# A gated linear scan with a top-2 mixture of adapters on one core: output rows of 8 KB, shorter early input rows, the masked logits on GpSimd, and a new order on every engine

## The chip, the cores and the metric

The kernel runs on one core of a Trainium2 chip. The metric is the time of one execution in device microseconds; the kernel before has a median of 201.33 us over three runs (201.27 to 201.44).

## The reference, cut to what matters

```python
# a, b: (8, 6400, 128) float32
h = zeros((8, 128))
for t in range(6400):                 # a linear scan along the sequence, per batch
    h = a[:, t] * h + b[:, t]
    x[:, t] = h
x = x.reshape(51200, 128)
logits = x @ w_gate                   # 8 experts
topk = argpartition(-logits, 2)[:, :2]
w = softmax of the two largest logits
out = x + sum over the two experts e of  w_e * ((x @ A[e]) @ B[e])    # rank 16
```

## The kernel before, in words

The 51200 tokens are 100 chunks of 512. `a` and `b` come from HBM with tokens on partitions; TensorE turns them so that the 128 features lie on partitions and the tokens along the row; VectorE runs the scan of a chunk along the row; TensorE multiplies with `A` and `w_gate`, the gate is worked out, and TensorE adds the chunk and its delta.

Each step has one letter, and the dictionary `ORDER` (line 24) spells out, for each engine, the order in which its steps are issued. No scheduler moves anything at run time: an engine issues its string from left to right and waits at each step for the semaphores of what that step needs. The steps are:

- **x, y (SyncE):** loads of `a` and `b`. `LOADS_A` (line 12) and `SEGMENTS` (line 11) give the chunks of each load. A load of m chunks lays 4m neighbouring tokens on one partition, so its rows in HBM are 2 KB times m: one chunk 2 KB, two chunks 4 KB, four chunks 8 KB. `a_tm` and `b_tm` hold 16 chunks each.
- **a, b, f (TensorE):** transposes of `a` (`solo_a`), of `b`, or of both together in alternation (f, in `front`). In the long middle part an f takes the `b` of chunk c and a half of two chunks of the `a` of the next four; `ahead` (line 415) says which. So the step f of chunk 88 needs the load of `a` of chunks 92 to 95.
- **a (ScalarE):** copies a transposed bank of `a` from PSUM to `a_st` (line 386).
- **s (VectorE):** the scan of one chunk, from `a_st` and from the PSUM bank of `b` (line 402), into `xT` in float16. The banks of `b` are `BANK_B` (line 16), the others rotate through `RING` (line 22).
- **z (TensorE, ScalarE):** `x @ [A, w_gate]` for up to three blocks of 128 tokens (line 500), copied to `zl` (line 506).
- **1 to 8, u, p, q, r:** the gate of a group of chunks (`GROUPS`, line 14; mostly six chunks), in `gating`: on VectorE the largest logit (1), its place (2), the logits with that place masked (3, line 536), the second largest (4) and its place (6); on GpSimd two differences (5, 8); on ScalarE one sigmoid (u); on GpSimd the two weights and their sum (p, q, r).
- **m (GpSimd or VectorE, as `MU` says, line 56):** the product of a chunk's `z` with its gate (line 588). **t (TensorE, then ScalarE or VectorE, as `TE` says, line 53):** the transpose of that product for two chunks and its copy (line 605).
- **d (TensorE), o (ScalarE):** chunk plus delta into PSUM (`out_chunk`, line 614), and the copy to `outt` (line 631), which holds 16 chunks.
- **o, p (SyncE):** the stores (`store`, line 648), with the chunks of `STORES` (line 13) in each. `BACKS` (line 20) says over how many chunks the tokens of an `xT` block are interleaved, which sets the row of a store: today 2 KB for the first and last four chunks, 4 KB for the rest. `SPLIT` (line 23) cuts one store in two by partitions.

All loads but one and all stores go through one queue, that of SyncE, in the order of its string. Where SyncE stands before a store that is not ready, the loads behind it are not issued.

Of the kernel before, what the change touches and what calls it, by code (L numbers as in the profile page):

```python
# [18 lines left out]
COLD, SOLO, FUSED, AE = {0: 1.95, 1: 1.3}, {1: 0.436, 2: 0.48}, {2: 0.59}, [0.592, 0.592]  # L19
BACKS = [1] * 4 + [2] * 46 + [1] * 4  # L20
ONE_SIGMOID, T_UNIT = True, 2
RING = [0, 3, 4, 5, 6, 7]
SPLIT = {20: [68]}
ORDER = {
    "pe": (
        "wbaabzzbazzbaaaazzaztffffzztzfdzzffzzfdfzfzzzffzzftzzffdzfdzzftzfzfzdfdzfzzzfzzfttzzffddtddzzfzfdzzf"
        "ztdffzzdtdffzztdzfdzzfdtzffzztddffzddtdffddzztzffzztzdffzdzztffzzzzdddtdtffzddztffzdzdfddfztzzffzdzd"
        "tffzzzddftzzzffdztzdftfddzftddffzzzdzfzdftzzffzztzddffdztzdtffzztddffddzzzfdzztzzfzdftzzfdtdffzzzddd"
        "ffdtztzffzzzddfdfttzdffazzdztdfddtzzzdzzddtafazdzzbtdzbzztddztdbzzadbdtddzdzdzttddtzddtdddtdtddddttd"
        "d"  # L30
    ),
    "act": (
        "ycciacazzazzuaaaazzuzaataaazztzzauaozzaazozaazzzzaazuatazzaoauzzoztzaazzaoazoazzzzzaauztzaaoooozzaza"
        "ozzazoaazzuootaazozzazoazozaazzutoaoazoouoaaoozzzaazztzoaazzozaazzzzooouoaazooztaazzoooaoazzzuaazzoo"
        "aazzzooazzzaaozztoautaoozaooaazzzoazzouazzaazzzooaaozztoaazzouoaaoozzzaozzzzzaoatzzauooaazzzoooaaozt"
        "zaauzzzaoooatzoaaazzuozooozzzoozzotaauzzzotozzzzoootzzauoouoozzotoztuoooztooooouuoooooo"
    ),
    "dve": (
        "ss12346ss123m4i61ss2s3s4s1s6s2s3s4s6s1s2s3s4s6sss1ss2s3s4sts16s2t3ss4sts1s62s3sts4sts1s263s4stssts6s"
        "ssts1s234tts1s263ss4ssts6sts1s2sts3s41s26s3sts4ss6sts1sts23sts4s6t1s2ssts13s4s2t6s3s4s6stss1s23sts4s"  # L40
        "m6tsts1m2m34s6ss1st12m3m4263s4ts1mm2m63m4mm6t1m21m32m34m4t66tmmtt"
    ),
    "pool": (
        "ccc85qpr85pqrmc855pqrmm8pqrmm85qprmmmm58mmqprmmmmm85mpqrmmmm85mmpqr58mmmmpmqmrmmmm85mmpqrmmm8m5mpqmr"
        "mmmmmm58qprmmm85mmmqprmmmmm58pmqrmmmmmm58pqrmm58mmmmqprmmmm58pqrmmm58qpmrmm58mq85prpq85pqrr8585ppqqr"
        "r"
    ),
    "sp": (
        "xxyxyxyxyxyxyyyxyyxyyxooyxyyoxyyyyyoxxoooyyxoyyyxoyxyooyyxoxopyoyyxoyyxyoooxyoyxyooyxyooyyxooyyxoyyx"
        "ooyxyoooyxoxxyyyoooyooooooooooooooooooo"  # L50
    ),
}
TE = (
    "aaaadaddaddaddadddadddaadddadddaddaadddaadadaadadddd"
)
MU = (
    "dpppppppppppppppppppppppppppppppppppppppppppppppppppppppppppppppppppppppppppdpdpdppppddpdddddddddddd"
# [144 lines left out]
def bass_associative_scan_2x2__then__mixture_of_adapters_kernel(  # L202
# [29 lines left out]
    with ExitStack() as stack:  # L232
# [54 lines left out]

        o_ms = P.add("pool", "c", [], lambda: eng["pool"].memset(ident_f[:, :], 0.0), dur=0.46)
# [20 lines left out]
        o_cB = P.add("pool", "c", [o_c[2]], lambda: eng["pool"].tensor_copy(B_h, cst_f[:, W:]), dur=0.38)  # L309

# [62 lines left out]
        def emptied(c, g, o, ba):  # L373
# [11 lines left out]
            e = P.add("act", "a", [o] + [ast_user[k % NA] for k in chunks] + [o_sg if c == 0 else None],  # L385
                      lambda: eng["act"].copy(dst, src()), dur=AE[0 if m == 1 else 1])  # L386
# [43 lines left out]
        def front(c):  # L430
# [3 lines left out]
            sl, q, m, h = place[0][c]  # L434
            if m == 1:
                solo_a(c, 0)
            elif (c - h, 0) not in o_A:
                for p in (0, 2):
                    for g in (0, 1):
                        solo_a(c - h + p, g)  # L440
            deps, ts = turned(1, c, bb)
            deps += user[bb.n]
            if c in ahead and place[0][c + 4][2] == 4:
                c1, g = ahead[c]
# [9 lines left out]
            elif c in ahead:  # L454
                if h % 2:
# [35 lines left out]
        def zlogits(b0, n):  # L491
# [10 lines left out]
            o = P.add("pe", "z", [scanned(b0 + n - 1), o_ch], zmm, dur=(0.059 if span[b0 // 4][1] == 1 else 0.062) * n, ring=bk, mm=n)  # L502
# [14 lines left out]
        def gating(gi, b0, nb):  # L517
# [17 lines left out]
            d3 = P.add("dve", "3", [d2],  # L535
                       lambda: eng["dve"].scalar_tensor_tensor(  # L536
                           out=ll, in0=kk1, scalar=-1.0e30, in1=Lp, op0=ALU.mult, op1=ALU.add),
                       dur=dur, lock=True)
# [20 lines left out]
            p1 = P.add("pool", "p", [a1, d2, d3] + free,  # L559
# [12 lines left out]
        def back(gi, c0, q0, n):  # L572
# [28 lines left out]
            te = "dve" if TE is None else {"a": "act", "d": "dve"}[TE[turn["t"]]]  # L601
# [12 lines left out]
        def out_chunk(c, e_t):  # L614
# [12 lines left out]
            o_D[c] = P.add("pe", "d", [e_t, o_cB], delta, dur=0.448 if span[c][1] == 1 else 0.48, ring=bo, mm=8, late=(1, [e_t, o_cB]))  # L627
            reads(b0, o_D[c])
            p0 = b0 % NO
            o_oe[c] = P.add("act", "o", [o_D[c]] + [out_user[p0 + k] for k in range(4)],  # L630
# [174 lines left out]
```

## Time and profile before

| | |
|---|---|
| time of the profiled execution | 201.33 us |
| its span, first to last instruction | 199.5 us |
| outside the span | 1.8 us |
| TensorE, VectorE, ScalarE, GpSimd busy | 91%, 89%, 89%, 64% |
| packets of SyncE's queue, as a share of 16 engines' span | 97.5% |
| bytes read and written in HBM | 52.56 MB, 26.21 MB |

The time is that of the execution from which the profile was taken, and it is also the median. The span is what the profile shows; the 1.8 us around it are the launch and the end. A busy share is the part of the span in which an engine has an instruction in work. The share of a queue is the time its packets took on the 16 DMA engines; where packets overlap, it goes over 100% in a stretch.

### The profile page before, as it was taken

Reading aid. Unit: us, or ns where it says so; the run is one execution under the profiler, and the core shown is the slowest. Engines: PE = TensorE matmul, PEld = TensorE weight load, DVE = VectorE, ACT = ScalarE, POOL = GpSimd, SP = SyncE. Lnnn points to the kernel's source line nnn. Section 1 sums busy time; section 2 is a strip of 40 time slices with the busy share of each in tenths; the row PEclk is TensorE's granted clock in tenths of the full one; section 3 lists DMA queues with packets and bytes.
Section 4 is the critical chain, followed back from the end, with each engine's and each line's share of the span. In section 5 each row is a group of like instructions: output and inputs, shape, how many; then the busy total and the mean of one; then the engine's idle time right before and its main releaser. Section 6 shows DMA issues by size and latency. Waiting matters only on the chain.

```text
span 199.5 us, 7518 instructions
## 1 busy us (share of the span) xinstructions
PE 181.4 (91%) x3137; PEld 165.1 (83%) x3137; DVE 177.8 (89%) x269; ACT 177.9 (89%) x384; POOL 128.2 (64%) x205
## 2 busy tenths in 40 slices
PE   2887988999999999999999989989999999898881
PEld 1766877888899999899998979978989899797770
DVE  0586789999999999999999988999999999999880
ACT  2476597999999999999999998989989999999872
POOL 1023006692798969966986794969888786665440
PEclk9995599999999999999999999999999999999999
DMA  6999999999999999999999999999999999999697
GB/s 185 401 405 415 414 412 413 414 414 404 419 410 420 409 416 418 410 420 407 420 413 407 415 418 417 419 411 418 417 408 418 411 409 407 412 389 369 268 365 272
DMA packets 21381, 79.26 MB, mean 397 GB/s; under 512 B 3427, under 2 KB 3555, under 8 KB 18403
## 3 DMA queue, kind: packets, MB, share of 16 engines
q1 hardware_dynamic: 19875, 78.39, 97.5%
q10 hardware_dynamic: 1472, 0.40, 0.9%
q8 instruction: 24, 0.39, 0.8%
q14 instruction: 10, 0.08, 0.1%
HBM read 52.56 MB, written 26.21 MB: 395 GB/s over the span
## 4 chain that ended last, share of the span: by engine, by line
PE 41%; DMA 23%; DVE 15%; ACT 13%; SPq 2%; issue 2%; POOL 2%; DVEq 0%; ACTq 0%
PE ps L768 22%; PE ps L772 19%; DMA a_tm<-in_a_dram 15%; DVE xT L402 9%; DMA b_tm<-in_b_dram 8%; ACT zl L506 4%; ACT outt L631 4%; ACT a_st L386 4%; DVE zw L588 4%; SPq L335 2%; ACT zwT L605 1%; DVE zwT L605 1%; POOL g L562 1%; DVE k L534 0%; DVE L L536 0%
## 5 line engine op out<-in xcount | busy, mean ns | idle before, releaser
L402 DVE TENSOR_TENSOR_SCAN xT<-a_st,xT,ps 128x512 f16<-128x512 f32 x96 | 120.1, 1251 | 7.1 <-PE ps L768 5.3
L588 POOL TENSOR_TENSOR zw<-zl,g 128x512 f16<-128x512 f32 x82 | 85.9, 1071 | 9.8 <-PE ps L768 8.3
L506 ACT COPY zl<-ps 128x408 f32<-128x408 f32 (+1 forms) x138 | 70.5, 629 | 4.7 <-PE ps L772 4.7
L768 PE MATMUL ps<-ident_f,b_tm 64*128 64x64 f32 (+1 forms) x768 | 67.1, 235 | 7.7 <-DVE xT L402 3.9
L386 ACT COPY a_st<-ps 128x512 f32<-128x512 f32 x100 | 64.3, 718 | 8.1 <-PE ps L768 7.9
L768 PE MATMUL ps<-ident_f,a_tm 64*128 64x64 f32 (+1 forms) x768 | 68.9, 236 | 0.8 <-DMA a_tm<-in_a_dram 0.8
L768 PEld LDWEIGHTS ps<-ident_f,b_tm 64*128 64x128 f32 (+1 forms) x768 | 55.9, 143 | 10.1 <-DMA b_tm<-in_b_dram 4.1
L631 ACT COPY outt<-ps 128x512 f32<-128x512 f32 x100 | 62.4, 714 | 1.8 <-PE ps L772 1.3
L768 PEld LDWEIGHTS ps<-ident_f,a_tm 64*128 64x128 f32 (+1 forms) x768 | 57.6, 144 | 6.5 <-ACT a_st L386 1.0
L772 PE MATMUL ps<-cst_h,zwT 128*128 128x128 f16 x400 | 56.0, 220 | 1.5 <-ACT zwT L605 0.8
L772 PE MATMUL ps<-ident_h,xT 128*128 128x128 f16 x400 | 57.4, 231 | 0.0
L772 PEld LDWEIGHTS ps<-ident_h,xT 128*128 128x128 f16 x400 | 49.7, 142 | 1.6
L772 PEld LDWEIGHTS ps<-cst_h,zwT 128*128 128x128 f16 x400 | 42.4, 107 | 2.7 <-ACT zwT L605 1.0
L772 PE MATMUL ps<-cst_h,xT 128*128 128x136 f16 x400 | 42.1, 234 | 0.7 <-DVE xT L402 0.4
L772 PEld LDWEIGHTS ps<-cst_h,xT 128*128 128x128 f16 x400 | 32.4, 145 | 3.8 <-DVE xT L402 1.0
L768 PE MATMUL ps<-ident_h,zw 128*128 128x128 f16 x400 | 31.7, 221 | 1.6 <-DVE zw L588 0.7
L768 PEld LDWEIGHTS ps<-ident_h,zw 128*128 128x128 f16 x400 | 24.4, 99 | 3.9 <-DVE zw L588 1.2
L605 ACT COPY zwT<-ps 128x1024 f16<-128x1024 f16 (+1 forms) x21 | 22.0, 1050 | 0.0
L605 DVE COPY zwT<-ps 128x1024 f16<-128x1024 f16 (+1 forms) x31 | 20.3, 656 | 0.3 <-PE ps L768 0.3
L542 POOL TENSOR_TENSOR dd<-m 128x24 f32<-128x24 f32 (+3 forms) x23 | 5.8, 251 | 17.4 <-DVE m L540 17.4
L562 POOL TENSOR_TENSOR g<-k,w 128x192 f32<-128x192 f32 (+3 forms) x23 | 10.7, 466 | 9.7 <-DVE k L547 7.5
L545 POOL TENSOR_TENSOR dd<-m 128x24 f32<-128x24 f32 (+3 forms) x23 | 6.2, 270 | 15.7 <-DVE m L540 15.7
(23 smaller groups left out, 87.3 us busy)
## 6 DMA issues: line engine op xcount, KB each, us to landing
a_tm<-in_a_dram SPq DMA_DIRECT2D x23, 1024.0 KB, 16.5
b_tm<-in_b_dram SPq DMA_DIRECT2D x46, 512.0 KB, 16.2
out_dram<-outt SPq DMA_DIRECT2D x45, 512.0 KB, 14.2
a_tm<-in_a_dram SPq DMA_DIRECT2D x8, 256.0 KB, 8.9
out_dram<-outt SPq DMA_DIRECT2D x8, 256.0 KB, 5.0
b_tm<-in_b_dram SPq DMA_DIRECT2D x7, 256.0 KB, 11.7
out_dram<-outt SPq DMA_DIRECT2D x1, 272.0 KB
b_tm<-in_b_dram ACTq DMA_DIRECT2D x1, 256.0 KB, 3.5
```

Source lines behind the costliest of these rows:

```text
L335: return eng[e].dma_start(tile[sl][:, q : q + m, :].rearrange("p h d -> p (h d)"), tokens(src, c, m, 4 * m).rearrange("p h d -> p (h d)"))
L386: lambda: eng["act"].copy(dst, src()), dur=AE[0 if m == 1 else 1])
L402: last = eng["dve"].tensor_tensor_scan(out=xT[:, xb, s0:s1], data0=a_st[:, c % NA, s0:s1], data1=ps[:, bk, s0:s1], initial=init, op0=ALU.m ...
L506: lambda: eng["act"].copy(zl[:, z0 : z0 + n, :].rearrange("p k w -> p (k w)"), ps[:, bk.n, 0 : n * W]),
L542: lambda: eng["pool"].tensor_tensor(out=vd, in0=v2, in1=v1, op=ALU.subtract), dur=0.186 + nb * 1.77e-3)
L545: lambda: eng["pool"].tensor_tensor(out=vr, in0=v1, in1=v2, op=ALU.subtract), dur=0.186 + nb * 1.77e-3)
L562: lambda: eng["pool"].tensor_tensor(out=gg, in0=kk2, in1=bc(u2), op=ALU.mult), dur=pd)
L588: lambda me=me, wv=wv, zv=zv, gv=gv: eng[me].tensor_tensor(out=wv, in0=zv, in1=gv, op=ALU.mult),
L605: f = (lambda: eng["act"].copy(dst, src())) if te == "act" else (lambda: eng["dve"].tensor_copy(dst, src()))
L631: lambda: eng["act"].copy(outt[:, p0 : p0 + 4, :].rearrange("p k d -> p (k d)"), ps[:, bo.n, :]), dur=0.6)
L768: return self.pe.transpose(*args)
L772: return self.pe.matmul(*args, **kwargs)
```

## The change

- **Stores.** Chunks 12 to 83 are stored four at a time with rows of 8 KB (18 stores) instead of two at a time with rows of 4 KB (36). The blocks of `xT` of these chunks are interleaved over four chunks instead of two, so a z or d of a block needs the scans of all four.
- **Loads.** `a` of chunks 4 to 11 comes in four loads of two chunks (4 KB rows) instead of two loads of four (8 KB rows). The step f of chunks 4 to 7 takes `a` of the chunk behind it, and four transposes of `a` stand alone (chunks 4, 9, 10, 11), as many as before (four, all of the first four-chunk load).
- **Masked logits.** The one VectorE step 3 becomes two GpSimd steps: 7 (the mask times -1e30, which stands in a new constant `big`) and 3 (plus the logits).
- **Who does what.** `MU` gives VectorE 23 products instead of 18, GpSimd 77 instead of 82. `TE` gives VectorE 30 copies of t instead of 31, ScalarE 22 instead of 21; and it has a second part, by which four of the 100 copies o go to VectorE (chunks 21, 62, 71 and 88).
- **Banks.** `BANK_B` has three PSUM banks instead of two, `RING` five instead of six.
- **Orders.** Every string of `ORDER` is new. In SyncE's, 62.39 MB go through the queue up to the end of the load of `a` of chunks 92 to 95, instead of 61.34 MB (counted in the string: 238 chunks of 256 KB instead of 234, the four more being outputs); 69.21 MB instead of 69.73 MB up to the last load of `b`; and 3.15 MB instead of 4.72 MB up to the last of the loads without which chunk 4 cannot be scanned.

```diff
-LOADS_A = [1] * 4 + [4] * 23 + [1] * 4
-STORES = [1] * 4 + [2] * 46 + [1] * 4
+LOADS_A = [1] * 4 + [2] * 4 + [4] * 21 + [1] * 4
+STORES = [1] * 4 + [2] * 4 + [4] * 18 + [2] * 6 + [1] * 4
-BANK_B = [1, 2]
+BANK_B = [0, 1, 2]
-BACKS = [1] * 4 + [2] * 46 + [1] * 4
+BACKS = [1] * 4 + [2] * 4 + [4] * 18 + [2] * 6 + [1] * 4
-RING = [0, 3, 4, 5, 6, 7]
-SPLIT = {20: [68]}
+RING = [3, 4, 5, 6, 7]
+SPLIT = {8: [68]}
...
+        o_big = P.add("pool", "c", [], lambda: eng["pool"].memset(big[:, :], -1.0e30), dur=0.1)
...
-                    ahead[c + i] = (c + 4 + 2 * (1 - i % 2), i // 2)
+                    ahead[c + i - 4] = (c + 2 * (1 - i % 2), i // 2)
...
-            if m == 1:
+            if c not in o_ae:
                 solo_a(c, 0)
-            elif (c - h, 0) not in o_A:
-                for p in (0, 2):
-                    for g in (0, 1):
-                        solo_a(c - h + p, g)
             deps, ts = turned(1, c, bb)
             deps += user[bb.n]
-            if c in ahead and place[0][c + 4][2] == 4:
-                c1, g = ahead[c]
+            m = place[1][c][2]
+            if m > 1 and (c in ahead or place[0][c + 1][2] == 2):
+                c1, g = ahead.get(c, (c + 1, 0))
...
-            d3 = P.add("dve", "3", [d2],
-                       lambda: eng["dve"].scalar_tensor_tensor(
-                           out=ll, in0=kk1, scalar=-1.0e30, in1=Lp, op0=ALU.mult, op1=ALU.add),
-                       dur=dur, lock=True)
+            d7 = P.add("pool", "7", [d2, o_big] + old,
+                       lambda: eng["pool"].tensor_tensor(out=ll, in0=kk1, in1=big[:, 0:1].unsqueeze(2).broadcast_to([128, nb, E]), op=ALU.mult), dur=pd)
+            d3 = P.add("pool", "3", [d7],
+                       lambda: eng["pool"].tensor_tensor(out=ll, in0=ll, in1=Lp, op=ALU.add), dur=pd)
...
+            oe = "act" if TE is None or "|" not in TE else {"a": "act", "d": "dve"}[TE.split("|")[1][c]]
+            f = (lambda: eng["act"].copy(dst, src())) if oe == "act" else (lambda: eng["dve"].tensor_copy(dst, src()))
```

More of the change, by code (lines that the diff above doesn't have):

```diff
@@ L51 @@
+        "oxxyyyoyooooooooooooooo"
     ),
@@ L453, in front @@
                 emptied(c1, g, o, ba)
-            elif c in ahead:
-                if h % 2:
+            elif m > 1:
+                if c in o_B:
                     return
@@ L558, in gating @@
             free = old + o_mulast.get(gi - NG, [])
-            p1 = P.add("pool", "p", [a1, d2, d3] + free,
+            p1 = P.add("pool", "p", [a1, d2, d7] + free,
                        lambda: eng["pool"].tensor_tensor(out=kk1, in0=kk1, in1=bc(u1), op=ALU.mult), dur=pd)
@@ L625, in delta @@
                 return last
-            o_D[c] = P.add("pe", "d", [e_t, o_cB], delta, dur=0.448 if span[c][1] == 1 else 0.48, ring=bo, mm=8, late=(1, [e_t, o_cB]))
+            o_D[c] = P.add("pe", "d", [e_t, o_cB], delta, dur=DD[span[c][1]], ring=bo, mm=8, late=(1, [e_t, o_cB]))
             reads(b0, o_D[c])
             p0 = b0 % NO
-            o_oe[c] = P.add("act", "o", [o_D[c]] + [out_user[p0 + k] for k in range(4)],
-                            lambda: eng["act"].copy(outt[:, p0 : p0 + 4, :].rearrange("p k d -> p (k d)"), ps[:, bo.n, :]), dur=0.6)
+            oe = "act" if TE is None or "|" not in TE else {"a": "act", "d": "dve"}[TE.split("|")[1][c]]
+            dst, src = outt[:, p0 : p0 + 4, :].rearrange("p k d -> p (k d)"), lambda: ps[:, bo.n, :]
+            f = (lambda: eng["act"].copy(dst, src())) if oe == "act" else (lambda: eng["dve"].tensor_copy(dst, src()))
+            o_oe[c] = P.add(oe, "o", [o_D[c]] + [out_user[p0 + k] for k in range(4)], f, dur=0.6 if oe == "act" else 0.664,
+                            alt=("act", 0.6, "dve", 0.664))
             bo.evac = o_oe[c]
@@ L667, in store @@
             o_st.extend(parts)
-        c0 = 0
+        nf, c0 = 0, 0
         behind, due = [], []
@@ L683, in bass_associative_scan_2x2__then__mixture_of_adapters_kernel @@
             for c in range(c0, c0 + n, step):
-                for k in range(c, c + step):
+                for k in range(nf, span[c + step - 1][0] + span[c + step - 1][1]):
+                    nf = k + 1
                     for i, near in ((0, 7), (1, 1)):
```

51 lines of the change are left out of this document (26 added, 25 removed).

## The prediction

> **What bounds the kernel now.** I read the page first, for busy shares and the DMA queue:
>
> ```profile
> PE 181.4 (91%) x3137; PEld 165.1 (83%) x3137; DVE 177.8 (89%) x269; ACT 177.9 (89%) x384; POOL 128.2 (64%) x205
> DMA packets 21381, 79.26 MB, mean 397 GB/s; under 512 B 3427, under 2 KB 3555, under 8 KB 18403
> q1 hardware_dynamic: 19875, 78.39, 97.5%
> a_tm<-in_a_dram SPq DMA_DIRECT2D x23, 1024.0 KB, 16.5
> out_dram<-outt SPq DMA_DIRECT2D x45, 512.0 KB, 14.2
> ```
>
> Nothing has much room: three engines near 90%, SyncE's queue at 97.5%. A load lands 16.5 us after its issue, so this queue is a long line, and its bytes decide when something lands, not its issue. The busy time by stretches says where each limit holds (columns: stretch, length, busy us of PE, PEld, DVE, ACT, POOL with instructions, clock, DMA share, GB/s):
>
> ```profile
> 12.00:17.00 5.00, 4.57 (x67) 3.78 (x65) 2.88 (x10) 3.42 (x9) 2.02 (x6) 0.74 1.03 420
> 17.00:34.00 17.00, 14.96 (x233) 13.05 (x231) 14.93 (x22) 11.93 (x27) 3.05 (x10) 0.78 1.02 412
> 34.00:100.00 66.00, 65.09 (x1243) 59.74 (x1245) 64.96 (x89) 66.00 (x146) 52.40 (x74) 1.00 1.02 414
> 100.00:155.84 55.84, 53.20 (x996) 48.85 (x993) 53.12 (x71) 53.68 (x116) 44.57 (x59) 1.00 1.02 415
> 155.84:183.70 27.86, 26.35 (x418) 24.73 (x419) 27.68 (x47) 27.30 (x59) 18.66 (x31) 1.00 1.01 401
> 183.70:190.30 6.60, 5.96 (x92) 5.48 (x93) 6.08 (x20) 6.03 (x13) 3.70 (x9) 1.00 0.67 263
> 190.30:194.70 4.40, 3.76 (x58) 3.17 (x55) 3.52 (x9) 3.13 (x8) 1.73 (x10) 1.00 1.02 401
> ```
>
> DMA stays full up to 183.7 us and has its one large hole after that, 6.60 x (1.02 - 0.67) = 2.3 us. VectorE is idle for 2.12 and 2.07 us in the first two stretches, for 0.18, 0.52 and 0.88 us in the last three. Then the chain that ended last, for the events behind these stretches (start, length, what), and VectorE's timeline for the first two and the last instruction of the end:
>
> ```profile
> 5.21 10.29 DMA a_tm<-in_a_dram
> ...
> 16.93 1.29 DVE xT L402
> ...
> 135.80 19.08 DMA a_tm<-in_a_dram
> ...
> 155.16 0.64 PE ps L768 x16
> ```
> ```profile
> 155.84 1.28 DVE L402 TENSOR_TENSOR_SCAN xT<-a_st,xT,ps 128x512 f16<-128x512 f32 x1 [0.38 <-PE ps L768]
> 157.04 0.33 DVE L534 TENSOR_TENSOR k<-zl,m 128x192 f32<-128x192 f32 x1
> 194.26 0.42 DVE L605 COPY zwT<-ps 128x512 f16<-128x512 f16 x1 [0.16 <-PE ps L768]
> ```
>
> Two landings gate the compute. The scan of chunk 4 at 16.93 waits for the `a` of chunks 8 to 11 (landed 15.5), because its step f carries that. And at 154.88 the last 1 MB load of `a`, chunks 92 to 95, lands; the f of chunk 88 starts at 155.16 and its scan at 155.84. From there VectorE works almost without a gap to 194.7: the end is 155.84 plus VectorE's remaining string.
>
> **The sum's base.** The profiled execution took 201.33 us, 1.8 us more than its span of 199.5; the median is the same 201.33, so differences in the span are taken one for one.
>
> **8 KB stores, 4 KB loads.** Stretches in which one row length prevails give its rate (same columns; loads of `a` in 8 KB rows, then stores in 4 KB rows, then stores in 2 KB rows):
>
> ```profile
> 55.50:59.50 4.00, 4.00 (x76) 3.56 (x70) 3.90 (x5) 4.00 (x11) 4.00 (x4) 1.00 1.01 412
> 191.00:194.50 3.50, 3.03 (x46) 2.65 (x47) 2.63 (x7) 2.43 (x7) 1.26 (x6) 1.00 1.02 404
> 195.50:198.00 2.50, 0.00 (x0) 0.00 (x0) 0.00 (x0) 0.43 (x1) 0.00 (x0) 1.00 1.03 385
> ```
>
> GB/s by share: 408, 396, 374. The stores of chunks 12 to 83 are 72 x 0.262 = 18.9 MB: 47.7 us at 396, 46.3 at 408, a gain of 1.4 us. The first stretch holds loads; no 8 KB store was traced, so the ends are 0 (such rows go as two packets; 8 KB loads do go as one, since 21381 - 18403 packets are not under 8 KB) and 1.4. I take 1.4, the rate being the queue's and not the direction's. `a` of chunks 4 to 11, 2.1 MB, goes the other way: +0.15. The queue's work falls by about 1.2 us. The Trainium skill (DMA: Bandwidth & Descriptors, Anatomy of one DMA) gives each DMA on the GpSimd path a fixed 2.0 us besides its bytes; 18 fewer stores would by that, as an estimate, save 36 us and give 165. The trace disagrees: at 97.5% of the engines' span there is no fixed part left to save, it is hidden behind the line.
>
> **The start.** Chunk 4 needs 3.15 MB through the queue instead of 4.72: 1.57 MB at 412 GB/s, 3.8 us earlier. That can recover up to the 4.2 us of VectorE's idle time at the start. I count it at nothing at the end, because the landing for chunks 92 to 95 covers it; without that gate it would be worth up to 3.8.
>
> **Work moved between engines.** Group rows (busy, mean ns):
>
> ```profile
> L536 DVE SCALAR_TENSOR_TENSOR L<-k,zl 128x192 f32<-128x192 f32 (+3 forms) x23 | 7.5, 326 | 0.2
> L562 POOL TENSOR_TENSOR g<-k,w 128x192 f32<-128x192 f32 (+3 forms) x23 | 10.7, 466 | 9.7 <-DVE k L547 7.5
> L564 POOL TENSOR_TENSOR g<-g,k 128x192 f32<-128x192 f32 (+3 forms) x23 | 11.3, 497 | 1.3
> L588 POOL TENSOR_TENSOR zw<-zl,g 128x512 f16<-128x512 f32 x82 | 85.9, 1071 | 9.8 <-PE ps L768 8.3
> L588 DVE TENSOR_TENSOR zw<-zl,g 128x512 f16<-128x512 f32 x18 | 13.0, 733 | 0.7 <-POOL g L564 0.7
> L605 ACT COPY zwT<-ps 128x1024 f16<-128x1024 f16 (+1 forms) x21 | 22.0, 1050 | 0.0
> L605 DVE COPY zwT<-ps 128x1024 f16<-128x1024 f16 (+1 forms) x31 | 20.3, 656 | 0.3 <-PE ps L768 0.3
> L631 ACT COPY outt<-ps 128x512 f32<-128x512 f32 x100 | 62.4, 714 | 1.8 <-PE ps L772 1.3 <-DMA out_dram<-outt 0.3
> ```
>
> VectorE loses step 3 (-7.5) and one copy t (-0.7), gains five products (5 x 0.733 = +3.7) and four copies o. An o on VectorE isn't traced; bounds are its 0.656 copy of PSUM and its 0.733 product of 512; I take 0.67, +2.7. Net -1.8. ScalarE: -4 x 0.714 + 1.05 = -1.8. GpSimd: steps 7 and 3 have the shapes of L562 and L564, +10.7 + 11.3, less 5 x 1.071: +16.6, to 145 us or 73%, still with room. So compute as a whole gets 1.8 us shorter on the two fullest engines; again nothing of it counts before the gate.
>
> **The gate and the end.** 62.39 MB instead of 61.34 go through the queue up to `a` of chunks 92 to 95: 1.05 MB at 415 GB/s is +2.5. Forty of the output chunks ahead of it are in 8 KB rows by then (40/72 x 1.4 = -0.8), the early `a` costs 0.15: it lands **+1.9** later, at 156.8. The f of chunk 88 stands at the same place behind it. From the scan of chunk 88 on VectorE's string has 64 steps instead of 73: three copies t less (-2.0), two products more (+1.5), two o more (+1.3), seven steps 3 less and three others of the gate of chunks 78 to 83 less, all done earlier. For these ten:
>
> ```profile
> L536 DVE SCALAR_TENSOR_TENSOR L<-k,zl 128x192 f32<-128x192 f32 x14 | 5.6, 401 | 0.1
> ```
>
> Two of the seven are of this size, the other five take (7.5 - 5.6)/9 = 0.21 each: -1.9; the three others are like the 0.33 of L534 at 157.04: -1.0. Sum -2.1, but an instruction starts 0.08 us before the last one's end (155.84 + 1.28 against 157.04), and 9 x 0.08 = 0.7 of that was overlap: **-1.4**. Of VectorE's idle time at the end, 0.18 and 0.52 stand before steps that now come at other places, and go (**-0.7**); the 0.88 are the last gate's own path and stay. Sum: 1.9 - 1.4 - 0.7 = -0.2, **201.1 us**.
>
> Banks: the third bank of `b` can take away TensorE's waits for scans, the fifth instead of sixth other bank adds waits for copies:
>
> ```profile
> PE ps L768 <- DVE xT L402: 4.0, 8, 0.9
> PEld ps L768 <- ACT a_st L386: 1.3, 2, 1.0
> ```
>
> I take both at nothing, since TensorE has 1.5 us free behind the gate; ends -1 and +1. A store of four waits for its last chunk, and with it the loads behind it in SyncE's string: covered by the 16 us of line. And an o has to wait for the landing of the four chunks 16 earlier (0.3 us today, in the row of L631): ends 0 and +1, taken at 0.
>
> **The rivals.** A is the sum above.
>
> B, DMA is the only bound: the waits behind the gate shrink more than I allow. For it: chunk 4 runs 3.8 us earlier, both full engines have 1.8 us less to do, and 69.21 instead of 69.73 MB lie before the last load of `b` (-1.3 us). Against it: VectorE's string behind the gate is fixed. The floor is the queue without its hole, -1.2 - 2.3 = -3.5; half of that gives **199.5**.
>
> C, slower: GpSimd is now in the middle of the gate's path, and it slows when VectorE multiplies beside it (GpSimd twice the same shape, beside and without VectorE's product):
>
> ```profile
> 183.77 0.82 POOL L562 TENSOR_TENSOR g<-k,w 128x64 f32<-128x64 f32 x1 [2.22 <-DVE k L547]
> 186.42 0.30 POOL L562 TENSOR_TENSOR g<-k,w 128x64 f32<-128x64 f32 x1
> ```
> ```profile
> 183.75 0.68 DVE L588 TENSOR_TENSOR zw<-zl,g 128x512 f16<-128x512 f32 x1
> ```
>
> One such meeting costs 0.52. The place is the gates of chunks 84 to 99, where VectorE has all 16 products (14 before). Between steps 2 and 4 VectorE has a scan and a copy or product, 1.2 + 0.6 = 1.8 us, as cover for 0.47 + 0.50; it decides when both meet a product (0.97 + 1.04 = 2.0, over 1.8) and when step 7 also queues behind a product of 1.071 on GpSimd. Two gates of six late by 1.0 each: A + 2.0 = **203.1**. Against it: the 64% leave GpSimd time. The Trainium skill (SBUF — State Buffer, SBUF: two separate sides) says that VectorE with two SBUF inputs and GpSimd take one port pair by an exclusive lock, for a whole instruction. The rows agree: 0.52 is most of the product's 0.68.
>
> **The numbers.** No difference means within 0.2%, 0.4 us, which a measurement can about tell. A has 0.46, with a range of its own of 200.3 to 201.9: faster 0.17, same 0.15, slower 0.14. B has 0.28, all faster; C 0.26, all slower. Faster 0.45, same 0.15, slower 0.40. Low 199.2 leaves out less than half of B, high 203.1 half of C.
>
> **What would show it.** In the changed kernel: stretches with 8 KB stores run at 408 GB/s by share or more; the scan of chunk 4 starts near 13 us; the load for chunks 92 to 95 lands near 156.8 and the scan of chunk 88 follows within 1 us; VectorE then needs about 37 us. If the scan of chunk 88 comes later than the landing by more than 1.5 us, compute and not the queue is the gate, and A and B are wrong. If DMA's hole is gone and the span falls by over 1.5 us, it is B. If VectorE waits at step 4 for GpSimd by over 1 us in all behind the gate, it is C.

## The result: 1.0% slower, outside the range

The changed kernel takes 203.43 us (median of four runs, 203.15 to 203.59), the kernel before beside it 201.36 us: a ratio of 1.0102, 95% interval 1.0089 to 1.0114. Forecast were 201.1 us and a range of 199.2 to 203.1. The profiled execution took 203.15 us, its span is 201.3 us (before 199.5).

The page after: busy shares, packets, SyncE's queue, and GB/s in 40 slices of 5 us:

```profile
PE 181.6 (90%) x3137; PEld 164.6 (82%) x3137; DVE 178.3 (89%) x254; ACT 178.3 (89%) x381; POOL 143.3 (71%) x247
GB/s 183 385 413 413 415 413 414 413 413 407 348 373 347 409 425 422 409 413 414 417 428 415 409 422 411 420 424 413 411 413 423 411 413 402 421 382 373 276 365 267
DMA packets 19076, 79.25 MB, mean 394 GB/s; under 512 B 3171, under 2 KB 3299, under 8 KB 14051
q1 hardware_dynamic: 17571, 78.39, 96.5%
```

The 8 KB stores do go as single packets (4352 fewer under 8 KB). GpSimd has the work that was expected, VectorE and ScalarE are not relieved at all. And the eleventh to thirteenth slice, 50 to 65 us, run at 348, 373 and 347 GB/s; there is no such hole before. The gate: the load of `a` for chunks 92 to 95 in the answer for its tile (its start, then its time to landing), VectorE's timeline at the scan of chunk 88 and at its end, and the chain of waits:

```profile
L340 SPq DMA_DIRECT2D a_tm<-in_a_dram x1: 1365/1365/1365, 138.3 to 138.3; - x1
DMA to landing us min/median/max: 20.7/20.7/20.7
```
```profile
13.42 4.10 DVE L407 TENSOR_TENSOR_SCAN xT<-a_st,xT,ps 128x512 f16<-128x512 f32 x3
...
23.42 1.28 DVE L407 TENSOR_TENSOR_SCAN xT<-a_st,xT,ps 128x512 f16<-128x512 f32 x1 [2.14 <-PE ps L773]
...
159.94 4.05 DVE L407 TENSOR_TENSOR_SCAN xT<-a_st,xT,ps 128x512 f16<-128x512 f32 x3 [0.21 <-PE ps L773]
...
196.38 0.76 DVE L606 COPY zwT<-ps 128x512 f16<-128x512 f16 x2 [0.32 <-PE ps L773]
```
```profile
107.74 20.56 DMA a_tm<-in_a_dram
...
130.09 21.19 DMA b_tm<-in_b_dram
151.33 0.73 PE ps L773 x13
```

The load lands at 138.3 + 20.7 = 159.0 instead of 154.88, 4.1 us later where +1.9 was forecast; the scan of chunk 88 follows at 159.94, 1.0 us behind it as before; VectorE then needs 37.19 us (38.84 before) and the span ends 4.17 us after VectorE (4.82 before). 4.1 - 1.65 - 0.65 = +1.8, the difference of the spans. So what follows chunk 88 became shorter by about as much as was forecast, 2.3 us against 2.1, and the question is why chunk 88 comes 4.1 us late.

The landing alone does not answer it. Ahead of this scan, VectorE stands for only 0.21 us (0.38 before), and the scan ahead of it, that of the second half of chunk 87, is already 3.6 us late (before, then after):

```profile
154.56 0.66 DVE L402 TENSOR_TENSOR_SCAN xT<-a_st,ps 128x256 f16<-128x256 f32 x1
158.18 0.66 DVE L407 TENSOR_TENSOR_SCAN xT<-a_st,ps 128x256 f16<-128x256 f32 x1
```

The chain does not pass through this load either, but through an earlier one, of `b` of chunks 84 and 85, which lands at 151.28, and from there through the copies of ScalarE.

### The profile page after: what moved, and what is told of

Its sections match the earlier page's. It is cut to its first block, busy times and chain, and to the rows that moved or that the text cites. A ratio compares the mean times of both kernels' runs of the same rounds, so it can differ in the third digit from the quotient of the medians.

```text
span 201.3 us, 7482 instructions
## 1 busy us (share of the span) xinstructions
PE 181.6 (90%) x3137; PEld 164.6 (82%) x3137; DVE 178.3 (89%) x254; ACT 178.3 (89%) x381; POOL 143.3 (71%) x247
## 4 chain that ended last, share of the span: by engine, by line
DMA 28%; ACT 27%; PE 19%; DVE 17%; SPq 3%; issue 3%; POOL 1%; ACTq 0%; DVEq 0%
DMA a_tm<-in_a_dram 17%; DMA b_tm<-in_b_dram 11%; PE ps L773 10%; DVE xT L407 9%; ACT zl L507 9%; PE ps L777 9%; ACT a_st L391 8%; ACT outt L633 7%; DVE zw L589 5%; SPq L340 3%; ACT zwT L606 3%; DVE zwT L606 1%; DVE k L548 0%; DVE m L532 0%; POOL g L563 0%
## 5 line engine op out<-in xcount | busy, mean ns | idle before, releaser
L589 POOL TENSOR_TENSOR zw<-zl,g 128x512 f16<-128x512 f32 x77 | 80.1, 1061 | 1.8 <-PE ps L773 0.6
L773 PE MATMUL ps<-ident_f,b_tm 64*128 64x64 f32 (+1 forms) x768 | 64.8, 233 | 2.1 <-DMA b_tm<-in_b_dram 1.7
L391 ACT COPY a_st<-ps 128x512 f32<-128x512 f32 x100 | 58.0, 629 | 9.5 <-PE ps L773 8.5
L507 ACT COPY zl<-ps 128x408 f32<-128x408 f32 (+1 forms) x138 | 63.4, 534 | 2.4 <-PE ps L777 2.2
L633 ACT COPY outt<-ps 128x512 f32<-128x512 f32 x96 | 56.0, 650 | 3.0 <-PE ps L777 2.2
L773 PEld LDWEIGHTS ps<-ident_f,b_tm 64*128 64x128 f32 (+1 forms) x768 | 54.9, 142 | 3.3 <-DMA b_tm<-in_b_dram 2.3
L777 PE MATMUL ps<-cst_h,zwT 128*128 128x128 f16 x400 | 55.1, 220 | 1.8 <-ACT zwT L606 1.3
L537 POOL TENSOR_TENSOR L<-k,big 128x192 f32<-128x192 f32 (+3 forms) x23 | 10.9, 474 | 21.0 <-DVE k L535 21.0
L606 ACT COPY zwT<-ps 128x1024 f16<-128x1024 f16 (+1 forms) x22 | 22.8, 1039 | 0.9 <-PE ps L773 0.8
L589 DVE TENSOR_TENSOR zw<-zl,g 128x512 f16<-128x512 f32 x23 | 15.6, 698 | 0.7 <-POOL g L565 0.7
## 6 DMA issues: line engine op xcount, KB each, us to landing
out_dram<-outt SPq DMA_DIRECT2D x18, 1024.0 KB, 20.7
```

The source lines that it names most:

```text
L391: lambda: eng["act"].copy(dst, src()), dur=AE[m // 4])
L507: lambda: eng["act"].copy(zl[:, z0 : z0 + n, :].rearrange("p k w -> p (k w)"), ps[:, bk.n, 0 : n * W]),
L537: lambda: eng["pool"].tensor_tensor(out=ll, in0=kk1, in1=big[:, 0:1].unsqueeze(2).broadcast_to([128, nb, E]), op=ALU.mult), dur=pd)
L589: lambda me=me, wv=wv, zv=zv, gv=gv: eng[me].tensor_tensor(out=wv, in0=zv, in1=gv, op=ALU.mult),
L606: f = (lambda: eng["act"].copy(dst, src())) if te == "act" else (lambda: eng["dve"].tensor_copy(dst, src()))
L633: f = (lambda: eng["act"].copy(dst, src())) if oe == "act" else (lambda: eng["dve"].tensor_copy(dst, src()))
```

## Experiments

The kernel before took between 201.28 and 201.39 us beside these runs; "ratio" is always to it. In the diffs of SyncE's string a is a load of `a`, b of `b`, o a store, with the first chunk.

### The hole at 55 us

**Loads ahead of the store of chunks 4 and 5.** In the changed kernel SyncE stands 12.4 us before this store, with the loads b34, a40, b36, b38 and a44 behind it (waits of SyncE; its timeline, start and length of a group of issues):

```profile
SPq L664 <- ACT outt L633: 52.1, 17, 12.4
```
```profile
39.33 13.66 SPq L664 DMA_DIRECT2D out_dram<-outt  x3
53.04 1.22 SPq L340 DMA_DIRECT2D b_tm<-in_b_dram  x1
```

```diff
-o2 o3 o4 b34 a40 b36 b38 a44 o6
+o2 o3 b34 a40 b36 b38 a44 o4 o6
```

> The changed kernel, with one store (chunks 4 and 5) moved in SyncE's order from ahead of five loads to behind them; nothing else differs. Theory T1 (the queue ran dry while SyncE stood before that store, and from there on all loads land late): the loads of the 50 to 68 us stretch are issued up to 12 us earlier, the hole goes, the load for chunks 92 to 95 lands about 2 us earlier (near 157) and the time is 201.0 to 201.8. If only the empty time of the DMA engines counts (0.6 us) and the slow packets behind it have another cause: 202.5 to 203.0. Theory T2 (GpSimd in the gate's path makes the end late): 203.2 to 203.6, no change.

202.49 us, ratio 1.0059 (1.004 to 1.0079), at the edge of the range for the empty time alone. The hole is gone and 0.9 us of the loss with it.

**The store of chunks 8 and 9 in one.**

```diff
-SPLIT = {8: [68]}
+SPLIT = {}
-o10 a48 p8 o12
+o10 a48 o12
```

> The changed kernel, but the store of chunks 8 and 9 goes as one DMA of 128 partitions instead of one of 68 and, four issues later, one of 60. Theory S: the parted store loads the DMA engines unevenly, and in the run with the loads ahead of the store of chunks 4 and 5 the next load of b landed 3.6 us behind it where 2.5 us of bytes lay between. Then the load of a for chunks 92 to 95 lands about 1.2 us earlier than 158.98, and the time is 202.2 +- 0.4. Rival: the parting is harmless (the engines even out again over the following loads); the time stays within 0.4 us of 203.4.

203.71 us, ratio 1.0108 (1.0084 to 1.0133): no gain. The parting is harmless. Both edits together:

> The changed kernel with both: the store of chunks 4 and 5 behind the four loads b34, a40, b36, b38 and a44, and the store of chunks 8 and 9 in one. Theory: the landing for chunks 92 to 95 is late by the dry queue (about 1 to 1.5 us) and by the parted store (about 1.2 us), and the end follows it; landing near 156.5, time 201.0 +- 0.5. If only the dry queue counts: 202.5, as with the order alone. If neither explains it (the end is compute's own, by banks or GpSimd): 202.5 or more, although the landing comes earlier.

202.2 us, ratio 1.0044 (1.0029 to 1.006); the interval overlaps that of the first edit alone, and the 201.0 of the theory is missed. This is the repaired kernel of the sections below.

**Two loads ahead instead of five.** Is it the empty line or the late loads? The store of chunks 8 and 9 goes in one here too.

```diff
-o2 o3 o4 b34 a40 b36 b38 a44 o6 o8
+o2 o3 b34 a40 o4 b36 b38 a44 o6 o8
-SPLIT = {8: [68]}
+SPLIT = {}
```

> The changed kernel with the store of chunks 8 and 9 in one, and the store of chunks 4 and 5 moved behind two of the loads only (b34 and a40, not b36, b38 and a44). SyncE still stands before it from about 41 to 52.5 us, but the line behind it ends 3.8 us later, near 58.7. Theory (the line runs nearly dry, and that costs the 2.1 us between 55 and 65 us): with nearly 6 us of line left, as in the kernel before at its own stop, the stretch keeps 410 GB/s and the time is that of the run with all four loads ahead, 202.2 to 202.6. Rival: the standing SyncE itself, or the late loads b36, b38 and a44, cost it: 203.0 to 203.6.

202.2 us, ratio 1.0042 (1.0029 to 1.0054). SyncE stands here until 51.86 us and b36, b38 and a44 are issued almost as late as in the changed kernel (52.3 to 54.1 instead of 54.8 to 55.8 us), but the stretch is whole. Busy time from 55 to 68 us (last column GB/s), in the changed kernel, the one before, and this one:

```profile
55.00:68.00 13.00, 13.00 (x265) 12.15 (x265) 12.90 (x16) 13.00 (x30) 11.74 (x17) 1.00 0.99 364
```
```profile
55.00:68.00 13.00, 13.00 (x252) 11.91 (x253) 12.89 (x18) 13.00 (x30) 12.07 (x16) 1.00 1.02 415
```
```profile
55.00:68.00 13.00, 13.00 (x269) 12.23 (x268) 12.90 (x16) 13.00 (x30) 11.74 (x17) 1.00 1.02 414
```

And the last DMA ahead of the stop, its start and its time to landing, in the same order:

```profile
L664 SPq DMA_DIRECT2D out_dram<-outt x2: 432/432/432, 39.3 to 39.8; - x2
DMA to landing us min/median/max: 15.0/15.1/15.1
```
```profile
L335 SPq DMA_DIRECT2D a_tm<-in_a_dram x1: 328/328/328, 45.2 to 45.2; - x1
DMA to landing us min/median/max: 14.6/14.6/14.6
```
```profile
L340 SPq DMA_DIRECT2D a_tm<-in_a_dram x1: 339/339/339, 43.7 to 43.7; - x1
DMA to landing us min/median/max: 15.0/15.0/15.0
```

The line ends at 54.9, 59.9 and 58.7 us. SyncE is back at 52.7, 54.6 and 51.9 us: 2.2 us of line left in the changed kernel, at least 5.3 (a store issued at 47.3 us has no landing in the records) and 6.8 us in the two without a hole. So the dry line costs (415 - 364)/415 x 13 = 1.6 us of queue from 55 to 68 us, and some 0.7 us more from 50 to 55 us (361 against 415 GB/s); taking it away gains 1.2 us of time. The other runs agree: the two with the same stop and the same line (the store in one, and the 4 KB rows below) have 369 and 365 GB/s from 55 to 68 us, the two with all five loads ahead 412 and 413.

### Parts of the change

**4 KB rows again**, each store of four as two at its place:

```diff
-STORES, BACKS = [1] * 4 + [2] * 4 + [4] * 18 + [2] * 6 + [1] * 4
+STORES, BACKS = [1] * 4 + [2] * 46 + [1] * 4
```

> The changed kernel, with the outputs of chunks 12 to 83 in 4 KB rows again: each store of four chunks becomes two stores of two at the same place in SyncE's order. By the prediction's rate (408 against 396 GB/s) this costs 1.4 us: 204.8. By the packet times of the two traces (8 KB against twice 4 KB saves 2 to 3%, of which the queue's sum shows 0.15 to 0.3 us): 203.4 to 203.8. If four-chunk blocks cost more through later waits than the rows bring: faster, 202.5 to 203.2.

203.82 us, ratio 1.0122 (1.0108 to 1.0136) against 1.0102 (1.0089 to 1.0114): the long rows bring some 0.4 us, near what the intervals can tell. Two stretches with such stores and no hole (100 to 120 and 120 to 140 us, before and then after) say the same, 414 and 416 against 418 and 417 GB/s:

```profile
100.00:120.00 20.00, 19.03 (x359) 17.38 (x355) 18.87 (x26) 19.59 (x43) 16.20 (x22) 1.00 1.02 414
120.00:140.00 20.00, 18.89 (x360) 17.52 (x356) 19.40 (x24) 18.85 (x41) 15.21 (x19) 1.00 1.02 416
```
```profile
100.00:120.00 20.00, 19.56 (x360) 17.68 (x358) 19.33 (x28) 19.40 (x42) 18.05 (x26) 1.00 1.02 418
120.00:140.00 20.00, 19.21 (x357) 17.66 (x356) 19.22 (x27) 19.30 (x43) 14.15 (x25) 1.00 1.02 417
```

**Step 3 back on VectorE**, right ahead of step 4:

```diff
-"pool" 7: L = mask * big;  "pool" 3: L = L + logits
+"dve" 3: L = mask * -1e30 + logits
```

> The changed kernel, with the masked logits back on VectorE as one step ahead of step 4, and without GpSimd's steps 7 and 3. T1: the time before the last big load is set by the queue and stays; behind it VectorE has 1.9 us more work, GpSimd less: 203.4 to 205. T2: the path of each gate is shorter by two GpSimd steps and two hand-overs, 201.5 to 202.8.

212.0 us, ratio 1.054 (1.0514 to 1.0565): both ranges are missed. In orders that were made without it, the step back on VectorE costs 8.6 us; where that time is lost was not followed further.

**The mask on GpSimd alone, in the kernel before.** 

```diff
-"dve" 3: L = mask * -1e30 + logits
+"pool" 7: L = mask * big;  "pool" 3: L = L + logits
```

> The kernel before with one part of the change alone: the masked logits (step 3) as the two GpSimd steps 7 and 3, set ahead of the differences of their gate and at most one product earlier; nothing else moved. VectorE loses 23 instructions, 7.5 us by their durations and about 6 by the time until the next one starts; GpSimd gains about 22 us, to 75%. If the landing of the load for chunks 92 to 95 and VectorE's string behind it set the end, only the steps behind the gate count: about 1.5 us faster, 199.5 to 200.3, if GpSimd keeps up. If GpSimd, now between steps 2 and 4, is late at the places that this order gives it, VectorE waits at step 4 and the time is above 203.

216.37 us, ratio 1.0739 (1.0708 to 1.077). Its waits, and the two of the changed kernel beside them:

```profile
POOL L L538 <- DVE k L536: 20.3, 9, 6.3
DVE m L542 <- POOL L L540: 20.2, 19, 2.5
```
```profile
POOL L L537 <- DVE k L535: 21.0, 18, 3.9
DVE m L541 <- POOL L L539: 0.7, 1, 0.7
```

With the old orders VectorE waits at step 4 for GpSimd, 20.2 us in 19 gates; with the new ones 0.7 us in one. So the wait that rival C named exists, and the new orders avoid it. That it comes by the slowing of GpSimd beside VectorE is not shown: the two steps take 491 and 517 ns on the mean here and 474 and 500 in the changed kernel, little less.

### The gate and the ring of outputs

**In the kernel before**, the load for chunks 92 to 95 later, behind o48 and o50, and earlier, ahead of o46:

```diff
-o46 b86 b88 a92 o48 o50 b90
+o46 b86 b88 o48 o50 a92 b90
```

> The kernel before, with one load moved in SyncE's order: the load of a for chunks 92 to 95 stands behind two stores of 512 KB instead of ahead of them, so that it lands about 2.5 us later (near 157.4). T1 (the end follows that landing): 203.3 to 204.0. If compute has slack there, 201.2 to 201.8.

Ratio 1.0144 (1.0097 to 1.0192), some 204.2 us: slower by 2.9 us (2.0 to 3.9), where the load was to come some 2.5 us later.

```diff
-o46 b86 b88 a92 o48
+b86 b88 a92 o46 o48
```

> The kernel before, with the store of chunks 46 and 47 (0.5 MB, 1.27 us) moved behind the load of a for chunks 92 to 95. If the end follows that landing here too, it lands at 153.6 instead of 154.88 and the time is 200.1 +- 0.4. If the landing was not the gate, or the next load of b takes its place, the time stays at 201.3 within 0.4.

206.06 us, ratio 1.0229 (1.0204 to 1.0254): the expectation missed. The wait that took over:

```profile
ACT outt L631 <- DMA out_dram<-outt: 5.9, 2, 5.7
```

`outt` holds 16 chunks, and the copy of chunk 62 cannot start before the store of chunk 46 has landed. So the order of loads and stores is bound from both sides.

**In the repaired changed kernel** the same load ahead of the store of chunks 48 to 51:

```diff
-b88 o48 a92 b90
+b88 a92 o48 b90
```

> The last kernel, and besides the load of a for chunks 92 to 95 is issued ahead of the store of chunks 48 to 51 (1 MB, 2.5 us of queue). If the end follows that landing, it comes 2.5 us earlier than there and the time falls by a further 1 to 2.5 us, to about 199.5; less than 2.5 because the b of chunks 90 and the later loads land as before or later. If compute sets the end before that landing, the time is that of the last kernel within 0.4 us.

203.24 us, ratio 1.0091 (1.0073 to 1.0109): 1 us slower than without, and neither a gain nor the same time, as was expected. ScalarE waits for the store now:

```profile
ACT outt L633 <- DMA out_dram<-outt: 1.1, 1, 1.1
```

Then with this store in two halves, the load ahead of both, or between them:

```diff
-b88 o48 a92 b90
+b88 a92 o48 o50 b90      (ahead of both)
+b88 o48 a92 o50 b90      (between)
```

> The changed kernel with the loads ahead of the store of chunks 4 and 5, the store of chunks 8 and 9 in one, the outputs of chunks 48 to 51 in two stores of 4 KB rows instead of one of 8 KB, and the load of a for chunks 92 to 95 ahead of both. Theory: two landings gate the end, that load (for the scan of chunk 88) and the store of chunks 48 to 51 (for the output copies of chunks 64 to 67, which reuse its buffers); with the load ahead of the whole quad it landed at 155.10 but the store at 157.61, and ScalarE waited for that. In pairs the first half of the store lands at 156.4 and is no longer late: the scan of chunk 88 comes at 156.2 to 157.5 and VectorE's 37 us and the rest follow as in the other runs: span 197.6 to 199.0, time 199.5 to 200.8, under both kernels. Rival: compute ahead of the scan is not ready before 159 whatever lands; time 202.2 +- 0.5.

202.72 us, ratio 1.006 (1.0046 to 1.0075): the theory's gain does not come.

> As the last one, but the load of a for chunks 92 to 95 goes between the two stores of chunks 48 and 50. Theory: it lands at 156.4, the first store at 155.2, neither store is late; scan of chunk 88 at 157.5, time 200.7 +- 0.5. Rival as before: 202.2 +- 0.5.

202.47 us, ratio 1.0061 (1.0047 to 1.0074). Its load and its scan of chunk 88:

```profile
L340 SPq DMA_DIRECT2D a_tm<-in_a_dram x1: 1682/1682/1682, 136.9 to 136.9; - x1
DMA to landing us min/median/max: 19.6/19.6/19.6
```
```profile
158.68 5.42 DVE L407 TENSOR_TENSOR_SCAN xT<-a_st,xT,ps 128x512 f16<-128x512 f32 x4
```

It lands at 156.5, the scan comes 2.2 us later, at 158.68, and its row names no idle time before it. In the run with two loads ahead it lands at 157.7 and the scan comes at 158.64. So with the queue repaired something besides this landing keeps chunk 88 at about 158.6 us. (No run of the changed kernel or of a version of it has this scan sooner than 158.57.)

### What keeps chunk 88 at 158.6

**Less on VectorE, less on ScalarE, products to GpSimd**, each in the repaired kernel (202.2 us). The first two leave out three quarters of the columns of the pieces named:

```diff
+products of chunks 50, 53, 56, 80, 82 and VectorE's output copies: 128 columns of 512   (first)
+output copies of chunks 50 to 61 on ScalarE: 128 columns of 512                         (second)
-MU: chunks 50, 53, 56 on "d"                                                            (third)
+MU: chunks 50, 53, 56 on "p"
```

> The changed kernel with the loads ahead of the store of chunks 4 and 5 and the store of chunks 8 and 9 in one (202.2 us alone), and besides VectorE does a quarter of each of the nine pieces of work that the change gave it: its products of chunks 50, 53, 56, 80 and 82 and its four output copies of chunks 21, 62, 71 and 88 have 128 instead of 512 columns (the rest of these is left out). That takes about 5 x 0.45 + 4 x 0.45 = 4 us off VectorE and changes no DMA. Theory V: with the queue repaired VectorE's own string is what keeps this kernel above the one before; the time falls by 1.5 to 4 us, to 198.2 to 200.7. Rival: ScalarE, TensorE or the landings hold the end; less than 0.5 us.

201.64 us, ratio 1.0012 (1.0002 to 1.0023): 0.6 us, but its scan of chunk 88 stays at 159.06; the gain lies in the tail.

> The same repaired kernel (202.2 us), VectorE's work whole, and instead ScalarE copies a quarter of the columns for the outputs of chunks 50 to 61 (12 copies, the rest of these is left out): some 12 x 0.3 = 3.6 us off ScalarE. Theory V (VectorE's string): less than 0.5 us. Rival (ScalarE's string is the bound): 1.5 to 3.6 us faster. If both this and the run with less on VectorE gain little, a landing or TensorE holds the end.

202.3 us, ratio 1.0046 (1.0029 to 1.0063): nothing.

> The same repaired kernel (202.2 us), with all of its work: the products of chunks 50, 53 and 56 go back from VectorE to GpSimd, where the kernel before has them. VectorE loses 3 x 0.62 = 1.9 us, GpSimd gains 3.2. Theory V: 0.5 to 1.9 us faster, 200.3 to 201.7. Rival: GpSimd, which is 90% busy between 50 and 120 us, becomes late with them and hands the delay to its later steps: no gain or a loss of up to 2 us.

202.15 us, ratio 1.0035 (1.0022 to 1.0049): nothing. Up to the scan of chunk 88 VectorE is busy 142.85 us in the repaired kernel, 140.94 in the first of these runs and 141.17 in the third, and the scan comes at 159.02, 159.06 and 158.57: waiting took the place of the work. But of what was taken away only one output copy lies between the scans of chunks 79 and 88. So VectorE's work before that, and ScalarE's copies of chunks 50 to 61, are not the bound; VectorE's last stretch was not relieved by any run.

**Less on TensorE**, with the late landing (two loads ahead, 202.2 us) and with the early one (the load between the stores, 202.47 us). Half of the matmuls of step d of chunks 40 to 59 are left out:

```diff
-                for k in range(4):
+                for k in range(2 if 40 <= c < 60 else 4):
```

> The changed kernel with the store of chunks 4 and 5 behind two of the loads and the store of chunks 8 and 9 in one (202.2 us alone, load of a for chunks 92 to 95 at 157.7), and besides TensorE leaves out half of step d for chunks 40 to 59, 80 matmuls of some 0.06 us: 4.8 us off TensorE ahead of the scan of chunk 88, no DMA and no other engine changed. Theory T: with the queue repaired two things stand equally late before that scan, the landing (157.7) and TensorE's own string. Then the landing still holds it: scan of chunk 88 at 158.3 to 158.7, time 201.6 to 202.2. Rival (TensorE's string alone is the bound): scan up to 3 us earlier relative to this run's own landing is not possible, so this run does not tell that apart; it is the partner of the next.

203.95 us, ratio 1.0101 (1.0077 to 1.0125).

> The same 4.8 us less on TensorE, but in the kernel whose load for chunks 92 to 95 stands between two stores of chunks 48 to 51 (202.5 us alone, landing at 156.4, scan of chunk 88 at 158.7). Theory T: with both relieved the scan of chunk 88 comes at about 157.3, 1 us behind the landing, and the time falls by 1.0 to 1.5 us to 201.0 to 201.5, more than from either alone. Rival: something else (VectorE, ScalarE, the start) holds the scan near 158.7 and the time at 202.2 to 202.5.

203.04 us, ratio 1.0087 (1.0074 to 1.01); scan of chunk 88 at 158.78. Both missed: with less work for TensorE the kernel became slower. The first had a lower granted clock at this place (last section), and so says little; in the second the scan did not move, and what it lost, 0.5 us, lies behind VectorE's end.

**All places from chunk 40 on as before.** All compute orders stay as changed.

```diff
-STORES, BACKS = [1] * 4 + [2] * 4 + [4] * 18 + [2] * 6 + [1] * 4
+STORES, BACKS = [1] * 4 + [2] * 4 + [4] * 7 + [2] * 28 + [1] * 4
-o40 b78 a84 b80 o44 b82 a88 b84 b86 b88 o48 a92 ...
+o40 b78 b80 a84 o42 o44 b82 b84 a88 o46 b86 b88 a92 o48 o50 ...
```

> The changed kernel with the store of chunks 4 and 5 behind two of the loads, the store of chunks 8 and 9 in one, and from the store of chunk 40 on SyncE's order of the kernel before, its outputs in pairs of 4 KB rows from there (8 KB rows only for chunks 12 to 39). All compute orders stay as changed. Theory Q: the rest of 0.9 us lies in the bytes that stand ahead of the loads from chunk 80 on (b of chunks 80 and 84 land 4 us later than before, a of chunks 92 to 95 2.8 us). With the old order they land within 0.5 us of before (b of 80 at 138.3, b of 84 at 145.8, a of 92 to 95 at 154.9); scan of chunk 88 at 155.8 to 157, and with the 41.4 us from that scan to the end of the span measured in the other runs the span is 197.2 to 198.4: time 199.0 to 200.3, under both kernels. Rival K: the compute orders of the changed kernel reach chunk 88 no earlier than 158.6, or its output copies wait for stores that land later; time 202.0 or more.

203.74 us, ratio 1.0118 (1.0101 to 1.0135). Its load, its scan of chunk 88, and the chain of waits ahead of it:

```profile
L340 SPq DMA_DIRECT2D a_tm<-in_a_dram x1: 2749/2749/2749, 136.1 to 136.1; - x1
DMA to landing us min/median/max: 19.3/19.3/19.3
```
```profile
160.05 4.04 DVE L407 TENSOR_TENSOR_SCAN xT<-a_st,xT,ps 128x512 f16<-128x512 f32 x3
```
```profile
145.80 0.36 DVE m L532
146.18 0.71 DVE k L535
146.96 0.52 POOL L L537
147.54 0.60 POOL L L539
148.14 2.05 POOL zw L589 x2
150.49 0.69 DVE outt L633
151.18 1.20 DVE xT L407
```

The load lands at 155.4, half a us from its old time, and chunk 88 still comes only at 160.05. The theory of late loads falls, its rival holds: the compute orders of the changed kernel do not reach chunk 88 before 158.6 us. (Its other arm, output copies that wait for stores, is small here, 0.9 us at one place.) The chain of this run goes without any DMA from 121 to 165 us, and through GpSimd at 147 to 150 us: the two mask steps, then two products, for which TensorE and an output copy wait. GpSimd from 140 to 145 us, before and after (fifth busy column):

```profile
140.00:145.00 5.00, 5.00 (x95) 4.55 (x93) 4.73 (x8) 4.79 (x10) 4.06 (x6) 1.00 1.03 417
```
```profile
140.00:145.00 5.00, 4.25 (x85) 3.86 (x80) 4.18 (x5) 4.18 (x11) 5.00 (x7) 1.00 1.00 411
```

It is the one engine that is full there, while TensorE, VectorE and ScalarE each have 0.7 us free or more. In the run above one wait of VectorE, 0.8 us ahead of the output copy, comes through it.

VectorE's own string is the other candidate, and its rows (third busy column) say more. Up to the scan of chunk 88, in the kernel before and with two loads ahead:

```profile
0.00:155.84 155.84, 144.68 (x2568) 131.28 (x2569) 140.51 (x196) 140.29 (x304) 104.08 (x158) 0.97 1.01 406
0.00:158.64 158.64, 146.33 (x2607) 132.60 (x2609) 142.74 (x190) 142.01 (x307) 117.14 (x194) 0.99 1.01 407
```

Six instructions fewer keep it busy 2.2 us longer. And from the scan of chunk 79 to that of chunk 88, in the kernel before and with the load between the two stores:

```profile
140.27:155.84 15.57, 15.01 (x282) 13.75 (x283) 14.86 (x21) 14.97 (x32) 12.88 (x19) 1.00 1.02 415
141.15:158.68 17.53, 16.48 (x301) 14.95 (x301) 16.84 (x24) 15.13 (x33) 15.58 (x24) 1.00 1.02 414
```

VectorE is idle for 0.7 us in both; the 2.0 us more are work: four copies t instead of two, one copy o, and one step 2 that takes 0.80 us where the next takes 0.36. It waits for TensorE three times there, 0.6 us in all, and never for GpSimd. (The chain of this run passes through the landing of `b` of chunks 80 and 81 at 142.48, but what VectorE waits for from there on is in these 0.6 us.) So steps that stood behind chunk 88 now stand ahead of it, and they are the larger part of its 2.8 us of delay in this run. That is read from the rows; no run set these steps back or gave GpSimd less to do at this place, so how the delay is shared between the two engines stays open. None of the versions beats the kernel before.

## Why the prediction was wrong, step by step

- **"Covered by the 16 us of line"** is the step that failed first. The wait of the store was named and the loads behind it too; the cover was read from the median time to landing. At this stop SyncE came back with 2.2 us of line, after which the queue ran at 364 GB/s for 13 us. Without it (two loads ahead) the time is 202.2 us: 1.2 of the 2.3 us between forecast and result. Not only the load that was taken for the gate lands later by it: `b` of chunks 84 and 85 comes at 151.28 in the changed kernel and at 149.85 with two loads ahead.
- **8 KB rows, -1.4 us and -0.8 up to the gate:** mis-sized. The rate rose by 0.2 to 1% and not by 3% (in the run with 4 KB rows it is 416 and 417 GB/s in these stretches), and the run with 4 KB rows gives some 0.4 us. It was the upper of the two ends that had been given, and the rate of a stretch of loads was taken for that of stores. The estimate by the Trainium skill (DMA: Bandwidth & Descriptors, Anatomy of one DMA), 36 us for 18 stores by the fixed 2.0 us that the page gives for the GpSimd path, was rightly set aside: that run has the 18 stores back and costs 0.4 us.
- **The landing, +1.9:** with the queue repaired it is +2.8 (157.7); the gain for the rows that did not come (0.8 at this point) is about the rest.
- **"Nothing of it counts before the gate"** and "the f of chunk 88 stands at the same place behind it" are the second failure, worth the other 1 us or so. They took for granted that compute would be ready when the load landed. A row of the prediction shows how little room there was: VectorE stood for 0.38 us ahead of chunk 88 in the kernel before. The steps that leave its string behind chunk 88 ("all done earlier") were taken off there and charged nowhere, and VectorE is busy 2.2 us longer ahead of that scan. The runs with the load at 156.5 and 155.4 show chunk 88 no earlier than 158.6 us. In the changed kernel and in the repaired one landing and compute are late together (0.21 us and no wait ahead of that scan), and so neither alone moves the time.
- **GpSimd "with room" at 73%** (71% measured) was a mean over the span; from 140 to 145 us it has none.
- **Work moved, -1.8 on VectorE and on ScalarE:** mis-sized; both gained 0.5 and 0.4 us of busy time. VectorE has 15 instructions less, and by the sum of their durations 1.4 us less to do (194.1 instead of 195.5), but an instruction that starts before the end of the last one counts its overlap only once; the prediction took this off behind the gate (0.08 us each) and not in the whole. ScalarE's groups overlap more: the copies a, z and o sum to 197.2 us before and 177.4 after in the rows of the page, in an engine that is busy 177.9 and 178.3 us, so such a row is no price of what an instruction less saves.
- **The start:** chunk 4 at 13.42, as said (near 13). Chunk 8 at 23.42 against 23.33 before, so nothing is left of it 10 us later: VectorE waits 2.14 us for TensorE there. The zero was right, but not for the reason given, the landing for chunks 92 to 95, which comes much later.
- **The tail:** 37.2 us where "about 37" was said (36.7 by the sum), and in part by luck. VectorE's work fell by 1.8 us (37.27 to 35.50 busy) and not by 1.4. Its idle time, which was to fall by 0.7, rose by 0.1. And the span ends 0.65 us sooner after VectorE, which the sum does not have.
- **Waits for the ring of outputs, taken at 0, end +1:** small in the changed kernel, but the reason why no load could be moved forward: 1.1 us in one run, 5.9 in the other.
- **The rivals:** the changed kernel comes out 0.3 us above C's 203.1, but not by C. Its own sign, a wait of more than 1 us at step 4, is not there (0.7 us over the whole span); the product that it saw as late on GpSimd is another matter, and open as said. B needed the hole in DMA at the end to shrink; the slices there still read 373 and 276 GB/s.

## What to carry to other kernels

A stop of the issuing engine is priced by the line that is left when it comes back (last landing ahead of the stop, less the time of the next issue), not by the median time from issue to landing. A landing that gates the compute is a bound only as long as compute is ready before it: before counting a later or earlier landing one for one, read when the engines would get there without it, and look at the engine's share in that stretch and not over the span. The idle time of the engine that the landing holds (0.38 us here) is all that can be put ahead of the gate for nothing: a step that leaves the end by being issued earlier has to be charged there. Where several limits are late together, taking away one shows nothing; the kernel that has all loads at their old places told more than the ones that moved one load.

## What the runs showed of the hardware

- After the queue had run nearly dry (engines busy for 0.75 of the time from 53 to 54 us) it was not back at full rate with the next issue: from 55 to 68 us the 16 engines were counted as busy for 0.99 of the time and moved 364 GB/s, against 414 and 415 with 5 us of line or more. Why the packets of that stretch take longer stays open.
- Two runs left out half of the matmuls of one step, and both were slower than without. In one of them TensorE's granted clock fell to 0.82 and 0.84 between 140 and 150 us; in the other, as idle at the same place, it stayed at 1.00. Whether idleness brought the clock down is not settled by two runs:

```profile
140.00:145.00 5.00, 3.56 (x44) 3.15 (x45) 3.61 (x4) 3.54 (x8) 5.00 (x7) 0.82 1.02 420
145.00:150.00 5.00, 5.00 (x88) 4.52 (x86) 3.38 (x5) 3.83 (x8) 3.57 (x5) 0.84 1.02 412
```
```profile
140.00:145.00 5.00, 3.53 (x60) 3.06 (x61) 3.96 (x5) 3.53 (x8) 5.00 (x7) 1.00 1.01 419
```
